# Fewer, longer rows for four small loads, and an earlier clearing of semaphores, in a gated attention and MLP decode kernel

## The chip, the core and the metric

The kernel runs on one core of one Trainium2 chip. A core has four compute engines, TensorE (PE, with its weight loads as PEld), VectorE (DVE), ScalarE (ACT) and GpSimd (POOL), a SyncE (SP) that here only issues transfers, and 16 transfer (DMA) engines that move data between the chip's memory and the on-chip buffer of 128 rows (partitions). Everything is 32-bit floating point. The metric is the device time of one execution in microseconds: the median of three runs, 677.85 us before the change (677.72 to 677.86).

## The reference

Two branches share one input of two rows of 448, and a sigmoid gate mixes them.

```python
B, Sq, D = 2, 1, 448          # H, Sk, Dh = 16, 4096, 256;  F = 1792
g = sigmoid((x * gate_w).sum(-1, keepdims=True))
q = (x @ wq).reshape(B, Sq, H, Dh).transpose(0, 2, 1, 3)
p = softmax(einsum("bhqd,bhkd->bhqk", q, k_cache) * Dh ** -0.5)
a = einsum("bhqk,bhkd->bhqd", p, v_cache).transpose(0, 2, 1, 3).reshape(B, Sq, H * Dh) @ wo
r = maximum(x @ w1 + b1, 0)
b = (r * r) @ w2 + b2
out = g * a + (1 - g) * b
```

K and V caches are 134 MB each, wq and wo 7.3 MB each, w1 and w2 3.2 MB each.

## The kernel before

**Rounds.** The 32 pairs of batch and head are worked through in 16 rounds of two heads of one batch. The tile of a round's K (or V) is 128 rows of 64 KB: 64 rows for each head, 64 keys in each row. VectorE multiplies a half of K's tile by q (`times_q`, L404) and sums over the 256 columns (`row_sums`, L409), half after half (`rest`); the maximum goes through TensorE and back (`maximum`, `softmax`), ScalarE takes the exponentials, and TensorE multiplies them with V (`values`) into a bank `po`. The first twelve rounds are a loop on TensorE; the last four are written out by hand (L599 to L661). K has two buffers, kp0 and kp1, and V one, vp; V of round 14 goes to kp0, which K no longer needs then.

**Output projection.** After each group of four heads (a unit), `turn_wide` transposes the heads' outputs through TensorE with the softmax sums folded in (`rl`), and `project` multiplies by wo. wo comes in four loads of four heads each (`load_wo`, L515). For heads 0 to 11 a load is 128 rows of 14336 bytes: a row holds eight successive rows of wo (`HJ` = 8) and the four heads lie in 32 rows each. The last four heads are two units of two heads, done by `turn_narrow` (L500) and `late_wo` (L529); their wo is laid out in 128 rows of two successive wo rows (`NJ` = 2) for each head, four pieces of 3584 bytes to a row. `late` (L526) spreads a product of two rows of 448 over four places of the bank `fin`.

**MLP.** w1 comes at the start; `ffn_turn` and `ffn_square` (L550 to L564) bring the hidden values into rows, add b1 from the tile `b1T` (128 rows of 14 values) and square them; w2 comes last of all, into kp1, in five pieces whose bounds are `W2_CUTS` (14 columns in all, each 1792 bytes of a row), and `late_w2` adds its products to `fin`.

**Start.** ScalarE issues x, gate_w, b2 and b1 (L292 to L295); x, gate_w and b2 lie at the front of kp1 until K of round 1 takes it. SP issues wq and K of round 0, then w1 and K of round 1.

**Order and waits.** `Flow` writes down every operation in program order with what it reads and writes, and derives the waits; each engine runs its own list in order. An operation that waits keeps everything behind it on the same engine waiting, and SP's loads are such a list. Loads have a semaphore of their own by name. `emit` (L118) allocates the semaphores, emits the engines' lists and, last on SP, behind an operation that waits for both output stores (L662), clears all semaphores in one instruction (L168).

**End.** On SP after K of round 15: V of round 14 (L624), wo of heads 12 to 15 (L636), V of round 15 in three pieces (L637, `V_CUTS`), w2 in five (L638). TensorE then does the values of round 14, `late_wo` of heads 12 and 13, the sums, the values of round 15, `turn_narrow` with the first w2 piece's products inside (L655), `late_wo` of heads 14 and 15 and the rest of w2; VectorE copies `fin` out and SP and ScalarE store one batch each (`store`, L615).

Of the kernel before, what the change touches and what calls it, by code (L numbers as in the profile page):

```python
# [23 lines left out]
class Flow:  # L24
# [7 lines left out]
    def __init__(self, nc):  # L32
        self.nc = nc
        self.eng = {PE: nc.tensor, ACT: nc.scalar, DVE: nc.vector, POOL: nc.gpsimd, SP: nc.sync}
        self.order = {e: [] for e in self.eng}
        self.ops = {}
        self.know = {e: {} for e in self.eng}
        self.seen = {}
        self.tokens = {}
        self.body, self.at, self.passes = None, 0, 0  # L40

    @staticmethod
    def span(r):
# [74 lines left out]
    def emit(self):  # L118
        nc = self.nc
        sems = {}  # L120
        counts = {}
        for proc, ops in self.ops.items():
            at = 0
            for o in ops:
                if proc not in self.eng:
                    o.inc = not o.give
                if o.inc and not o.give:
                    at += 1 if proc in self.eng else 16
                counts[id(o)] = at
        assert all(not t for t in self.tokens.values())  # L130

        def sem(name):
            if name not in sems:
                sems[name] = nc.alloc_semaphore(f"s_{name}")
            return sems[name]

        for proc in self.ops:
            sem(proc)
        for t in self.tokens:
            sem(t)  # L140

        def one(o):
            e = self.eng[o.eng]
            for t, n in o.takes:
                e.wait_ge(sem(t), n).then_inc(sem(t), -n)  # L145
            for p in o.waits:
                e.wait_ge(sem(p.proc), counts[id(p)])  # L147
            i = o.fn()
            n = 1 if o.proc in self.eng else 16
            if o.give:  # L150
                i.then_inc(sem(o.give), n)
            elif o.inc:
                i.then_inc(sem(o.proc), n)

        for eng in (POOL, DVE, ACT, SP, PE):
            for o in self.order[eng]:
                if isinstance(o, Op):
                    one(o)
                else:
                    passes, body, slot = o  # L160
                    with nc.Fori(0, passes, engines=bass.OrderedEngineSet([TYPES[PE]]),
                                 head_slot=None if slot is None else {TYPES[PE]: slot}):
                        for p in body:
                            one(p)
            if eng == SP:
                nums = sorted(s.num for s in sems.values())
                assert nums == list(range(nums[0], nums[0] + len(nums)))
                nc.sync.sem_clear(range(nums[0], nums[0] + len(nums)))  # L168


def gated_mix_kernel(nc, x, k_cache, v_cache, wq, wo, w1, b1, w2, b2, gate_w, out):
    P = 128
    B, H, S, DH = k_cache.shape
    D = x.shape[-1]
# [14 lines left out]
    NQ = N // QB  # L189
    assert QB == 2 * DH  # L190
    DQ = D // 4
    W2_CUTS = (2, 8, 11, 13)
    V_CUTS = (32, 56)
    LEAD = 4
    HJ = HG * DH // P
    HP = P // HG
    HN = HG * DH
    HALF = J * DH
# [3 lines left out]
    op = flow.op  # L202

    def sb(name, *shape):
        return nc.alloc_sbuf_tensor(name, shape, F32).ap()
# [12 lines left out]
    rs_t = [sb(f"rs{n}", P, B * HG) for n in range(2)]  # L218
    eo = sb("eo", P, 2)
    m16 = sb("m16", P, 4 * HG)  # L220
    xT = sb("xT", P, 2, XC, 2, B)
    z = sb("z", B, 1)
    g = sb("g", B, 1)
# [12 lines left out]
    rc = sb("rc", P, HG, B)  # L236
    rl_t = [sb(f"rl{n}", P, HG * B, 2) for n in range(2)]
    oTw = sb("oTw", P, HJ, B)
    oTn = [sb(f"oTn{n}", P, NJ, 2 * B) for n in range(2)]

    po_t = [bank(f"po{n}") for n in range(2)]
    acc = bank("acc")
# [3 lines left out]
    sm = bank("sm")  # L246
# [5 lines left out]
    def load(eng, sem, dst, src, w, r=(), give=None):  # L252
        e = flow.eng[eng]
        op(eng, lambda: e.dma_start(dst, src), r=r, w=w, dma=sem, give=give)  # L254

    def place(t, lo=0, hi=NK * DH):
        return ("vp" if t is vp else "kp1" if t is kp[1] else "kp0", lo, hi)
# [29 lines left out]
    def at_start(k, n=1):  # L287
        return place(kp[1], k * D, (k + n) * D)
# [3 lines left out]
    load(ACT, "x", x2, x.rearrange("b s d -> b (s d)"), [at_start(0)])  # L292
    load(ACT, "gw", gw, gate_w[None, :].to_broadcast([B, D]), [at_start(1)])
    load(ACT, "b2", b2r, b2[None, :].to_broadcast([B, D]), [at_start(2)])
    load(ACT, "b1", b1T, b1.rearrange("(p c) -> p c", c=FC), ["b1T"])  # L295

    v_, s_, t_, g_ = nc.vector, nc.scalar, nc.tensor, nc.gpsimd

# [7 lines left out]
    def vec(fn, r, w, give=None):  # L306
        op(DVE, fn, r=r, w=w, give=give)
# [10 lines left out]
    vec(lambda: v_.tensor_reduce(eo, ident.rearrange("p (a s) -> p s a", s=2), axis=AX.X, op=ALU.add), ["ident"], ["eo"])  # L318
    vec(lambda: v_.tensor_reduce(m16, ident.rearrange("p (r k) -> p k r", r=4)[:, :4 * HG, :], axis=AX.X, op=ALU.add),
        ["ident"], ["m16"])  # L320

    xr = start_at[:, 4 * D:].rearrange("b (k r s) -> b k r s", k=XC, s=2)
    for s in range(2):
# [6 lines left out]
    def mms(calls):  # L330
        def run():
            for out_, lhsT, rhs, start, stop in calls:
                i = t_.matmul(out_, lhsT, rhs, start=start, stop=stop, skip_group_check=True)  # L333
            return i
        return run
# [24 lines left out]
    op(PE, mms([(sm[:, :2 * B], ones_pp[:B, :], gd.rearrange("k s b -> k (s b)"), True, True)]), r=["ones", "gd"], w=["sm"])  # L360
    vec(lambda: v_.tensor_copy(gP, sm[:, :2 * B].rearrange("p (s b) -> p s b", b=B)), ["sm"], ["gP"])
    op(PE, mms([(acc[:B, :D], gd[:, 1, :], b2r, True, False)]), r=["gd", at_start(2)], w=["acc"])

    load_k(0)

# [117 lines left out]
    def turn_wide(u):  # L483
# [12 lines left out]
        for k in range(HG):  # L496
            at = slice(k * HP, (k + 1) * HP)
            op(ACT, lambda k=k, at=at: s_.activation(oTw[at], ptv[at, :, B * k:B * k + B], AF.Copy), r=["sm"], w=[("oTw", k, k + 1)])  # L498

    def turn_narrow(u, between=lambda: None):  # L500
        ptv = sm[:, :NJ * 2 * B].rearrange("p (j c) -> p j c", c=2 * B)
        a = u - NG + 1
        po, name, rl, oT = po_t[u % 2], f"po{u % 2}", rl_t[u % 2], oTn[a]
        o = shared[:, a * 512:(a + 1) * 512]
        op(ACT, lambda: s_.activation(o, po, AF.Copy), r=[name], w=[("shared", a * 512, (a + 1) * 512)])
        between()
        ov = o.rearrange("r (s p j) -> r s j p", s=2, j=NJ)
        op(PE, mms([(ptv[:, j, :], ov[:, s, j, :], rl[:, :2 * B, s], s == 0, s == 1) for j in range(NJ) for s in range(2)]),
           r=[("shared", a * 512, (a + 1) * 512), f"rl{u % 2}"], w=["sm"])
        op(ACT, lambda: s_.activation(oT, ptv, AF.Copy), r=["sm"], w=[f"oTn{a}"])  # L510

    wo_v = wo.rearrange("(h p j) n -> p h (j n)", p=P, j=NJ)
    wo_g = wo.rearrange("(g p j) n -> g p (j n)", p=P, j=HJ)

    def load_wo(u):  # L515
        if u < NG - 1:
            load(SP, "wo", wo_t, wo_g[u], ["wo"])
        else:
            load(SP, "wo", wo_t.rearrange("p (h k) -> p h k", h=HG), wo_v[:, u * HG:(u + 1) * HG, :], ["wo"])

    def project(u):
        t = wo_t.rearrange("p (j n) -> p j n", j=HJ)
# [3 lines left out]
    def late(lt, rhs, start=False, stop=False):  # L526
        return [(fin[32 * k:32 * k + B, :DQ], lt, rhs[:, k * DQ:(k + 1) * DQ], start, stop) for k in range(4)]

    def late_wo(h):  # L529
        u, k = unit_of[h]  # L530
        t = wo_t.rearrange("p (h j n) -> p h j n", h=HG, j=NJ)
        calls = []
        for j in range(NJ):
            calls += late(oTn[u - NG + 1][:, j, B * k:B * k + B], t[:, h % HG, j, :])
        op(PE, mms(calls), r=[f"oTn{u - NG + 1}", "wo"], w=["fin"])

    w2_t = kp[last % 2][:, :FC * D].rearrange("p (c n) -> p c n", n=D)
    w2_v = w2.rearrange("(p c) n -> p c n", c=FC)
# [89 lines left out]
    softmax(i + 1)  # L628
    times_q(i + 2, 0, LEAD, J)
    values(i, vt)  # L630
    turn_narrow(NG - 1)

    i = last - 1
    vt = vt_next
    rest(i + 1, 0, J)
    load_wo(NG - 1)  # L636
    vt_next = load_v(i + 1, vp, V_CUTS)  # L637
    load_w2()  # L638
    values(i, vt, 0, NK // 4)
# [3 lines left out]
    y0 = sb("y0", P, DQ)  # L643
    vec(lambda: v_.tensor_copy(y0, fin[:, :DQ]), ["fin"], ["y0"])
    store(y0, "y0")
    late_wo(H - 4)
    late_wo(H - 3)
    sums(NG)
    norm(NG)

# [1 line left out]
    at = [0, *(c // 2 for c in V_CUTS), NK // 2]  # L652
    for lo, hi in zip(at, at[1:]):
        values(last, vt, lo, hi)
    turn_narrow(NG, lambda: late_w2(0, W2_CUTS[0]))  # L655
    late_wo(H - 2)
    late_wo(H - 1)
    late_w2(W2_CUTS[0], FC)
    y4 = shared[:, :DQ]
    vec(lambda: v_.tensor_copy(y4, fin[:, :DQ]), ["fin"], [("shared", 0, DQ)])  # L660
    store(y4, ("shared", 0, DQ))  # L661
    op(SP, lambda: nc.sync.nop(), r=["out0", "out1"])  # L662
    flow.emit()


# [24 lines left out]
```

## Time and profile before

| What | us |
|---|---|
| median of three runs (lowest, highest) | 677.85 (677.72, 677.86) |
| the profiled execution's own time | 677.82 |
| its span on the core | 676.5 |
| VectorE, TensorE, ScalarE busy in it | 570.2, 245.4, 42.3 |

Times in the profile count from the start of the span; what the profiled execution took beyond its span, 1.32 us, lies around it. In a timeline a row is: start, duration, engine, line, operation, output<-input, shape and count, and in brackets how long the engine had been idle and what ended that. An engine's name with q (SPq, ACTq) is its sequencer, here issuing a transfer. In the groups by line a row has the count, then the busy time in all and the mean of one in ns, then the idle time before. In a table of stretches a row has the bounds, the length, busy time and count for each engine, the granted TensorE clock, the mean busy share of the 16 transfer engines (above 1 where packets overlap) and the rate. q1 is SP's queue of transfers, q10 ScalarE's, q8 the one that brings instructions. Where all matmuls go through one helper they have one line, L333, and are told apart by their tiles.

### The profile page before, as it was taken

How to read it: one execution, taken by the hardware profiler on the slowest of the kernel's cores; microseconds unless marked ns; L12 is line 12 of the kernel's file. 1: busy time of each engine (PE TensorE's matmuls, PEld its weight loads, DVE VectorE, ACT ScalarE, POOL GpSimd, SP SyncE). 2: the span in 40 equal slices, each digit the busy share in tenths (PEclk: the TensorE clock that was granted, in tenths of full speed). 3: DMA queues.
4: the chain of work that ended last, by engine and by line, in shares of the span. 5: the costliest groups of instructions: out<-in, count | busy, mean ns of one | idle time of the engine just before them, and what ended most of it. 6: DMA issues, size and time to landing. Idle time of an engine off the chain costs nothing.

```text
span 676.5 us, 3789 instructions
## 1 busy us (share of the span) xinstructions
PE 245.4 (36%) x1658; PEld 83.3 (12%) x1658; DVE 570.2 (84%) x143; ACT 42.3 (6%) x141; POOL 0.7 (0%) x6
## 2 busy tenths in 40 slices
PE   2522350502305761140505456050411580412476
PEld 1100210100001410010101411010100140100122
DVE  3069999999999895979979896897979899999920
ACT  0001000010100201010000201000010110000000
POOL 0000000000000000000000000000000000000000
PEclk9957585655758577585756678575665765675889
DMA  9999999999999999999999999999999999999997
GB/s 381 426 438 435 435 434 434 434 434 434 434 434 434 419 435 434 434 434 434 434 434 434 457 431 434 434 434 434 430 434 430 401 460 434 434 434 434 392 439 304
DMA packets 7062, 289.71 MB, mean 428 GB/s; under 512 B 902, under 2 KB 1036, under 8 KB 1932
## 3 DMA queue, kind: packets, MB, share of 16 engines
q1 hardware_dynamic: 6880, 289.54, 99.3%
q8 instruction: 8, 0.13, 0.1%
q10 hardware_dynamic: 172, 0.02, 0.0%
q14 instruction: 2, 0.02, 0.0%
HBM read 289.56 MB, written 0.01 MB: 428 GB/s over the span
## 4 chain that ended last, share of the span: by engine, by line
DMA 48%; DVE 31%; PE 3%; SPq 1%; issue 0%; DVEq 0%
DMA kp<-in_A_k_cache_dram 32%; DVE s L409 15%; DVE kp L404 15%; DMA vp<-in_A_v_cache_dram 11%; DMA kp<-in_B_w_dram 5%; PE po L333 3%; SPq L254 1%; PE fin L333 0%; PE mt L333 0%; DVE shared L660 0%; DVEq L147 0%; DVE nb L431 0%
## 5 line engine op out<-in xcount | busy, mean ns | idle before, releaser
L404 DVE TENSOR_TENSOR kp<-kp,q 128x8192 f32<-128x8192 f32 (+2 forms) x34 | 278.2, 8183 | 57.6 <-DMA kp<-in_A_k_cache_dram 57.6
L409 DVE TENSOR_REDUCE s<-kp 128x32 f32<-128x8192 f32 x32 | 278.0, 8686 | 1.1
L333 PE MATMUL po<-vp,pw 128*16 128x512 f32 (+1 forms) x960 | 135.8, 728 | 233.0 <-PEq L145 208.9
L333 PEld LDWEIGHTS po<-vp,pw 128*16 128x16 f32 (+1 forms) x960 | 31.1, 110 | 333.5 <-issue 307.3
L333 PE MATMUL mt<-ident,m 128*64 128x64 f32 x64 | 7.3, 318 | 141.3 <-PEq L145 87.4
L333 PE MATMUL sm<-rl,shared 128*128 128x8 f32 (+1 forms) x112 | 23.6, 347 | 9.2 <-ACT shared L489 8.1
L333 PE MATMUL acc<-wo,oTw 128*2 128x448 f32 x48 | 24.8, 683 | 2.5 <-ACT oTw L498 2.5
L333 PEld LDWEIGHTS sm<-rl,shared 128*128 128x128 f32 x112 | 23.0, 311 | 10.8 <-DVE rl L462 4.6
L450 ACT ACTIVATE pw<-zero 128x128 f32<-128x128 f32 x12 | 3.7, 312 | 325.5 <-PE po L333 325.5
L333 PEld LDWEIGHTS mt<-ident,m 128*64 128x64 f32 x64 | 4.8, 191 | 155.0 <-issue 99.0
L438 ACT ACTIVATE pw<-s,nb 64x64 f32<-64x64 f32 x32 | 11.1, 348 | 169.8 <-DVE nb L431 169.6
L660 DVE COPY shared<-fin 128x112 f32<-128x112 f32 x1 | 0.3, 275 | 20.8 <-PE fin L333 20.8
L333 PE MATMUL ph<-vp,xT 128*4 128x448 f32 x28 | 8.2, 759 | 15.6 <-DMA vp<-in_B_w_dram 15.6
L333 PE MATMUL po<-kp,pw 128*8 128x512 f32 x64 | 9.4, 744 | 8.8 <-DMA kp<-in_A_v_cache_dram 8.8
L333 PE MATMUL pq<-qs,sel 128*64 128x256 f32 x48 | 12.3, 594 | 0.0
L431 DVE TENSOR_REDUCE nb<-mt 128x1 f32<-128x64 f32 x16 | 3.6, 224 | 9.8 <-PE mt L333 9.8
L333 PE MATMUL po<-vp,xT 128*4 128x512 f32 x56 | 8.7, 787 | 4.9 <-DMA vp<-in_A_wq_dram 4.9
L460 DVE RECIPROCAL rc<-sm 128x8 f32<-128x8 f32 (+1 forms) x5 | 1.0, 196 | 7.7 <-PE sm L333 7.7
L380 ACT ACTIVATE q<-pq 128x256 f32<-128x256 f32 x16 | 6.1, 383 | 21.0 <-PE pq L333 20.7
L489 ACT ACTIVATE shared<-po 128x512 f32<-128x512 f32 x12 | 6.5, 591 | 11.4 <-PE sm L333 11.4
L333 PEld LDWEIGHTS acc<-wo,oTw 128*2 128x2 f32 x48 | 4.5, 98 | 20.6 <-issue 17.8
L438 ACT ACTIVATION_READ_ACCUMULATOR pw<-s,nb 64x1 f32 x32 | 5.9, 184 | 0.0
(65 smaller groups left out, 66.2 us busy)
## 6 DMA issues: line engine op xcount, KB each, us to landing
vp<-in_A_wq_dram SPq DMA_DIRECT2D x1, 7168.0 KB, 19.4
wo<-in_A_wo_dram SPq DMA_DIRECT2D x4, 1792.0 KB, 45.2
vp<-in_A_v_cache_dram SPq DMA_DIRECT2D x1, 4096.0 KB, 24.8
vp<-in_B_w_dram SPq DMA_DIRECT2D x1, 3136.0 KB, 18.0
vp<-in_A_v_cache_dram SPq DMA_DIRECT2D x1, 3072.0 KB, 31.7
kp<-in_B_w_dram SPq DMA_DIRECT2D x1, 1344.0 KB, 37.1
vp<-in_A_v_cache_dram SPq DMA_DIRECT2D x1, 1024.0 KB, 33.7
kp<-in_B_w_dram SPq DMA_DIRECT2D x2, 448.0 KB, 33.5
```

The lines of the kernel that those rows point to most:

```text
L254: op(eng, lambda: e.dma_start(dst, src), r=r, w=w, dma=sem, give=give)
L333: i = t_.matmul(out_, lhsT, rhs, start=start, stop=stop, skip_group_check=True)
L380: op(ACT, lambda: s_.activation(t, pq[:, :DH], AF.Copy), r=["pq"], w=[f"q{i % 3}"])
L404: vec(lambda: v_.tensor_tensor(kt, kt, q.unsqueeze(1).to_broadcast([P, hi - lo, DH]), op=ALU.mult), at + [f"q{i % 3}"], at)
L409: vec(lambda: v_.tensor_reduce(s[:, at], rows(t)[:, at, :], axis=AX.X, op=ALU.add), [place(t, half * HALF, (half + 1) * HALF)], [(f"s{i % ...
L431: vec(lambda: v_.tensor_reduce(nb, mt[:, :PH], axis=AX.X, op=ALU.max, negate=True), ["mt"], [f"nb{i % 2}"])
L438: op(ACT, lambda: s_.activation(pw[at, :, 2 * c:2 * c + 2], s[at].rearrange("p (m s) -> p m s", s=2), AF.Exp, bias=nb[at], accum_out=rs[at ...
L450: op(ACT, lambda: s_.activation(at, zero.unsqueeze(2).unsqueeze(3).to_broadcast([P, NK // 2, 2, 2]), AF.Copy), r=["zero"], w=[("pw0", 2 * ...
L460: vec(lambda: v_.reciprocal(c, sm[:, :B * n].rearrange("p (k b) -> p k b", b=B)), ["sm"], ["rc"])
L489: op(ACT, lambda s=s, lo=lo: s_.activation(o_w[:, s], pv[:, s, lo:lo + HJ // 2].unsqueeze(2).to_broadcast([P, HJ // 2, HG, HP]), AF.Copy), ...
L660: vec(lambda: v_.tensor_copy(y4, fin[:, :DQ]), ["fin"], [("shared", 0, DQ)])
```

## The change

Four parts:

- wo of heads 12 and 13 is loaded by itself, as 64 rows of 14336 bytes, in the layout of the earlier units (`load_wo`, u = 3). A new `turn_half` transposes these two heads into 64 rows (`oT2`), and `late_half` multiplies: eight steps on 64 rows instead of four on 128. wo of heads 14 and 15 keeps its layout and goes to kp1 behind w2's place (`wo_e`), free once the first half of K of round 15 has been reduced.
- b1 is loaded as 16 rows of 448 bytes to the front of kp1; one matmul with a mask `e16` repeats each row over eight partitions, and VectorE picks each partition's 14 values with a second mask `m_i` (a product and a sum) into `b1T`.
- w2 comes in four pieces, of 8, 3, 2 and 1 columns, and all its products come after those of wo.
- All semaphores but those of the two output stores are cleared while the stores are under way; ScalarE counts up a marker, `acted`, as its last instruction, which SP waits for; the stores' own two semaphores are waited for and counted down behind it.

```diff
-        for proc in self.ops:
-            sem(proc)
+        ends = [p for p in self.ops if p in self.last]
+        for proc in self.ops:
+            if proc not in ends:
+                sem(proc)
         for t in self.tokens:
             sem(t)
+        sem("acted")
+        inner = sorted(s.num for s in sems.values())
+        assert inner == list(range(inner[0], inner[0] + len(inner)))
+        for proc in ends:
+            sem(proc)
...
+            if eng == ACT:
+                nc.scalar.nop().then_inc(sem("acted"), 1)
             if eng == SP:
-                nums = sorted(s.num for s in sems.values())
-                assert nums == list(range(nums[0], nums[0] + len(nums)))
-                nc.sync.sem_clear(range(nums[0], nums[0] + len(nums)))
+                nc.sync.wait_ge(sem("acted"), 1)
+                nc.sync.sem_clear(range(inner[0], inner[0] + len(inner)))
+                for proc in ends:
+                    n = 16 * len(self.ops[proc])
+                    nc.sync.wait_ge(sem(proc), n).then_inc(sem(proc), -n)
...
-    W2_CUTS = (2, 8, 11, 13)
+    W2_CUTS = (8, 11, 13)
...
-    load(ACT, "b1", b1T, b1.rearrange("(p c) -> p c", c=FC), ["b1T"])
+    BR = 16
+    BI = P // BR
+    b1_at = 4 * D + XC * P
+    b1r = kp[1][:BR, b1_at:b1_at + BI * FC]
+    e16 = kp[1][:BR, b1_at + BI * FC:b1_at + BI * FC + P]
+    b1w = kp[1][:, b1_at + BI * FC + P:b1_at + 2 * BI * FC + P]
...
+    load(ACT, "b1", b1r, b1.rearrange("(r n) -> r n", r=BR), [b1r_at])
...
+    vec(lambda: v_.tensor_reduce(m_i, ident.rearrange("p (a i) -> p i a", i=BI), axis=AX.X, op=ALU.add), ["ident"], ["m_i"])
+    vec(lambda: v_.tensor_copy(e16.rearrange("r (a i) -> r a i", i=BI), ident[:BR, :BR].unsqueeze(2).to_broadcast([BR, BR, BI])),
+        ["ident"], [e16_at])
...
+    op(PE, mms([(ph[:, :BI * FC], e16, b1r, True, True)]), r=[e16_at, b1r_at], w=["ph"])
+    vec(lambda: v_.tensor_tensor(b1w.rearrange("p (c i) -> p c i", i=BI), ph[:, :BI * FC].rearrange("p (i c) -> p c i", i=BI),
+                                 m_i.unsqueeze(1).to_broadcast([P, FC, BI]), op=ALU.mult), ["ph", "m_i"], [b1w_at])
+    vec(lambda: v_.tensor_reduce(b1T, b1w.rearrange("p (c i) -> p c i", i=BI), axis=AX.X, op=ALU.add), [b1w_at], ["b1T"])
...
+    def turn_half():
+        u = NG - 1
+        ptv = sm[:PH, :HJ * 2 * B].rearrange("p (j c) -> p j c", c=2 * B)
+        po, rl = po_t[u % 2], rl_t[u % 2]
+        o_h = shared.rearrange("r (s j k p) -> r s j k p", s=2, j=HJ, k=2)
+        pv = po.rearrange("r (s p j) -> r s j p", s=2, j=HJ)
+        for s in range(2):
+            op(ACT, lambda s=s: s_.activation(o_h[:, s], pv[:, s].unsqueeze(2).to_broadcast([P, HJ, 2, HP]), AF.Copy),
+               r=[f"po{u % 2}"], w=[("shared", s * HN // 2, (s + 1) * HN // 2)])
+        ov = o_h.rearrange("r s j k p -> r s j (k p)")
+        op(PE, mms([(ptv[:, j, :], ov[:, s, j, :], rl[:, :2 * B, s], s == 0, s == 1) for j in range(HJ) for s in range(2)]),
+           r=["shared", f"rl{u % 2}"], w=["sm"])
+        for k in range(2):
+            at = slice(k * HP, (k + 1) * HP)
+            op(ACT, lambda k=k, at=at: s_.activation(oT2[at], ptv[at, :, B * k:B * k + B], AF.Copy), r=["sm"], w=[("oT2", k, k + 1)])
...
+    wo_e = kp[last % 2][:, FC * D:FC * D + 2 * NJ * D].rearrange("p (h j n) -> p h j n", h=2, j=NJ)
...
         if u < NG - 1:
             load(SP, "wo", wo_t, wo_g[u], ["wo"])
+        elif u < NG:
+            load(SP, "wo", wo_t[:PH], wo_g[u, :PH], ["wo"])
         else:
-            load(SP, "wo", wo_t.rearrange("p (h k) -> p h k", h=HG), wo_v[:, u * HG:(u + 1) * HG, :], ["wo"])
+            load(SP, "wo_e", wo_e.rearrange("p h j n -> p h (j n)"), wo_v[:, H - 2:, :], [wo_e_at])
...
+    def late_half():
+        t = wo_t[:PH].rearrange("p (j n) -> p j n", j=HJ)
+        calls = []
+        for j in range(HJ):
+            calls += late(oT2[:, j, :], t[:, j, :])
+        op(PE, mms(calls), r=["oT2", "wo"], w=["fin"])
...
-    turn_narrow(NG - 1)
+    turn_half()
...
     load_wo(NG - 1)
+    load_wo(NG)
     vt_next = load_v(i + 1, vp, V_CUTS)
     load_w2()
...
-    late_wo(H - 4)
-    late_wo(H - 3)
+    late_half()
...
-    turn_narrow(NG, lambda: late_w2(0, W2_CUTS[0]))
-    late_wo(H - 2)
-    late_wo(H - 1)
-    late_w2(W2_CUTS[0], FC)
+    turn_narrow(NG)
+    late_wo(0)
+    late_wo(1)
+    late_w2(0, FC)
...
-    op(SP, lambda: nc.sync.nop(), r=["out0", "out1"])
```

More of the change, by code (lines that the diff above doesn't have):

```diff
@@ L40, in __init__ @@
         self.body, self.at, self.passes = None, 0, 0
+        self.last = ("out0", "out1")
     @staticmethod
@@ L220, in gated_mix_kernel @@
     m16 = sb("m16", P, 4 * HG)
+    m_i = sb("m_i", P, 8)
     xT = sb("xT", P, 2, XC, 2, B)
@@ L238, in gated_mix_kernel @@
     oTw = sb("oTw", P, HJ, B)
-    oTn = [sb(f"oTn{n}", P, NJ, 2 * B) for n in range(2)]
+    oT2 = sb("oT2", P // 2, HJ, B)
+    oTn = sb("oTn", P, NJ, 2 * B)
     po_t = [bank(f"po{n}") for n in range(2)]
@@ L294, in gated_mix_kernel @@
     load(ACT, "b2", b2r, b2[None, :].to_broadcast([B, D]), [at_start(2)])
-    load(ACT, "b1", b1T, b1.rearrange("(p c) -> p c", c=FC), ["b1T"])
+    BR = 16
[4 more added lines that the diff above has]
+    b1w = kp[1][:, b1_at + BI * FC + P:b1_at + 2 * BI * FC + P]
+    b1r_at = place(kp[1], b1_at, b1_at + BI * FC)
+    e16_at = place(kp[1], b1_at + BI * FC, b1_at + BI * FC + P)
+    b1w_at = place(kp[1], b1_at + BI * FC + P, b1_at + 2 * BI * FC + P)
+    load(ACT, "b1", b1r, b1.rearrange("(r n) -> r n", r=BR), [b1r_at])
     v_, s_, t_, g_ = nc.vector, nc.scalar, nc.tensor, nc.gpsimd
@@ L498, in turn_wide @@
             op(ACT, lambda k=k, at=at: s_.activation(oTw[at], ptv[at, :, B * k:B * k + B], AF.Copy), r=["sm"], w=[("oTw", k, k + 1)])
+    def turn_half():
[13 more added lines that the diff above has]
+            op(ACT, lambda k=k, at=at: s_.activation(oT2[at], ptv[at, :, B * k:B * k + B], AF.Copy), r=["sm"], w=[("oT2", k, k + 1)])
     def turn_narrow(u, between=lambda: None):
         ptv = sm[:, :NJ * 2 * B].rearrange("p (j c) -> p j c", c=2 * B)
[L502 to L505, printed above, removed]
+        po, name, rl = po_t[u % 2], f"po{u % 2}", rl_t[u % 2]
+        o = shared[:, 512:1024]
+        op(ACT, lambda: s_.activation(o, po, AF.Copy), r=[name], w=[("shared", 512, 1024)])
         between()
@@ L508, in turn_narrow @@
         op(PE, mms([(ptv[:, j, :], ov[:, s, j, :], rl[:, :2 * B, s], s == 0, s == 1) for j in range(NJ) for s in range(2)]),
-           r=[("shared", a * 512, (a + 1) * 512), f"rl{u % 2}"], w=["sm"])
-        op(ACT, lambda: s_.activation(oT, ptv, AF.Copy), r=["sm"], w=[f"oTn{a}"])
+           r=[("shared", 512, 1024), f"rl{u % 2}"], w=["sm"])
+        op(ACT, lambda: s_.activation(oTn, ptv, AF.Copy), r=["sm"], w=["oTn"])
     wo_v = wo.rearrange("(h p j) n -> p h (j n)", p=P, j=NJ)
     wo_g = wo.rearrange("(g p j) n -> g p (j n)", p=P, j=HJ)
+    wo_e = kp[last % 2][:, FC * D:FC * D + 2 * NJ * D].rearrange("p (h j n) -> p h j n", h=2, j=NJ)
+    wo_e_at = place(kp[last % 2], FC * D, FC * D + 2 * NJ * D)
+    assert FC * D + 2 * NJ * D <= HALF
     def load_wo(u):
@@ L527, in late, with late_wo @@
         return [(fin[32 * k:32 * k + B, :DQ], lt, rhs[:, k * DQ:(k + 1) * DQ], start, stop) for k in range(4)]
-    def late_wo(h):
-        u, k = unit_of[h]
-        t = wo_t.rearrange("p (h j n) -> p h j n", h=HG, j=NJ)
+    def late_half():
[4 more added lines that the diff above has]
+        op(PE, mms(calls), r=["oT2", "wo"], w=["fin"])
+    def late_wo(k):
         calls = []
         for j in range(NJ):
-            calls += late(oTn[u - NG + 1][:, j, B * k:B * k + B], t[:, h % HG, j, :])
-        op(PE, mms(calls), r=[f"oTn{u - NG + 1}", "wo"], w=["fin"])
+            calls += late(oTn[:, j, B * k:B * k + B], wo_e[:, k, j, :])
+        op(PE, mms(calls), r=["oTn", wo_e_at], w=["fin"])
     w2_t = kp[last % 2][:, :FC * D].rearrange("p (c n) -> p c n", n=D)
```

## The prediction

> **What bounds the kernel now.** I read the page first, its slices and its queues.
>
> ```profile
> span 676.5 us, 3789 instructions
> PE 245.4 (36%) x1658; PEld 83.3 (12%) x1658; DVE 570.2 (84%) x143; ACT 42.3 (6%) x141; POOL 0.7 (0%) x6
> DMA  9999999999999999999999999999999999999997
> DMA packets 7062, 289.71 MB, mean 428 GB/s; under 512 B 902, under 2 KB 1036, under 8 KB 1932
> q1 hardware_dynamic: 6880, 289.54, 99.3%
> q8 instruction: 8, 0.13, 0.1%
> ```
>
> The transfer engines are at nine tenths or more in 39 slices of 40. The load queue q1 alone keeps them occupied for 99.3% of 676.5 us, that is 671.8 us, while VectorE, the busiest compute engine, has 570 us of work. So the kernel is bound by its loads: a change counts if it shortens or stalls that stream, or the work behind its last byte. Two stretches show the full rate and the end of the stream; the columns after the four engines' busy times are POOL, the TensorE clock, the DMA share and GB/s.
>
> ```profile
> 60.00:226.00 166.00, 50.37 (x370) 18.72 (x370) 159.68 (x37) 9.53 (x36) 0.00 (x0) 0.61 1.00 434
> 670.00:674.00 4.00, 3.14 (x112) 2.02 (x100) 0.00 (x0) 0.00 (x0) 0.00 (x0) 1.00 0.60 234
> ```
>
> Steady loading runs at 434 GB/s. In the last stretch 234 GB/s x 4 us = 936 KB still move, which is 2.16 us of full rate. The tail, in order of time, shows what follows:
>
> ```profile
> 666.10 0.20 PEld L333 LDWEIGHTS po<-vp,pw 128*8 128x8 f32 x8 [0.66 <-DMA vp<-in_A_v_cache_dram]
> 667.30 0.60 ACT L505 ACTIVATE shared<-po 128x512 f32<-128x512 f32 x1 [17.94 <-PE po L333]
> 669.38 0.95 PE L333 MATMUL fin<-wo,oTn 128*2 128x112 f32 x32 [0.27 <-ACT oTn L510]
> 670.47 1.33 PE L333 MATMUL fin<-kp,hT 128*2 128x112 f32 x48
> 673.28 0.86 PE L333 MATMUL fin<-kp,hT 128*2 128x112 f32 x24 [0.38 <-DMA kp<-in_B_w_dram]
> 673.77 0.11 PEld L333 LDWEIGHTS fin<-kp,hT 128*2 128x2 f32 x8 [0.19 <-DMA kp<-in_B_w_dram]
> 674.21 0.28 DVE L660 COPY shared<-fin 128x112 f32<-128x112 f32 x1 [20.80 <-PE fin L333]
> 674.51 0.51 SPq L254 DMA_DIRECT2D out_dram<-shared  x1
> ```
>
> TensorE waits for the last w2 piece until 673.77; then come eight matmuls, one copy and the store. The 2.16 us of bytes end at 673.77 rather than 672.16, so a mean transfer engine is done up to 1.6 us before the last one. The q8 row fits: 0.1% of 16 engines' span for eight instruction packets is 676.5 x 0.001 x 16 / 8 = 1.4 us per packet (0.7 to 2.0 by its rounding), and each sits on one engine. It is the last engine that sets the end.
>
> The end itself is in two rows, the final wait and the clear, and in the wait for the stores:
>
> ```profile
> L662 SPq EVENT_SEMAPHORE  x1: 17/17/17, 676.4 to 676.4; - x1
> L168 SPq EVENT_SEMAPHORE_RANGE_CLEAR  x1: 78/78/78, 676.4 to 676.4; - x1
> SPq L662 <- DMA out_dram<-shared: 1.3, 1, 1.3
> ```
>
> **The packets.** Bytes stay the same; rows get longer. wo of heads 12 and 13 goes from 2 x 128 rows of 3584 bytes to 64 of 14336: 192 packets fewer. w2's first two pieces become one: 128 fewer. b1 goes from 128 rows to 16: 112 fewer. Completion packets: one w2 load less, one wo load more, nothing. That is 432 packets, 27 per engine. The price of a packet is not in the trace directly, so I bound it: 289.54 MB at 434 GB/s is 667.1 us, q1 was occupied for 671.8, and the 4.7 us between, over 6880/16 = 430 packets, give at most 11 ns each. The other bound is nothing, since the next packet may be fetched under the one before. So 0 to 27 x 11 ns = 0.30 us. I take 0.20, nearer the upper end, because little but the packets can fill the 4.7 us.
>
> **The 64-row load.** It moves half of a wo load.
>
> ```profile
> wo<-in_A_wo_dram SPq DMA_DIRECT2D x4, 1792.0 KB, 45.2
> b1T<-in_B_b_dram ACTq DMA_DIRECT2D x1, 7.0 KB, 30.3
> ```
>
> 896 KB are 0.918 MB, 2.11 us at 434 GB/s. No load of this size on half of the rows stands in the trace; the nearest short ones, x, gate and b2 on two rows, say nothing of its rate. Bounds: it runs at the full rate (0), or at half of it (2.11 us more, less what the early engines absorb). I take 0, by the nearest row, wo's other loads, which lie within the full rate; the other end is the first rival. [...]
>
> **The extra work on chip.** The rows around it:
>
> ```profile
> 629.03 8.68 DVE L404 TENSOR_TENSOR kp<-kp,q 128x8192 f32<-128x8192 f32 x1
> 631.49 1.29 SPq L254 DMA_DIRECT2D vp<-in_A_v_cache_dram  x3
> 631.49 0.60 ACT L505 ACTIVATE shared<-po 128x512 f32<-128x512 f32 x1 [17.71 <-PE po L333]
> 632.23 1.08 PE L333 MATMUL sm<-rl,shared 128*128 128x4 f32 x8 [0.82 <-ACT shared L505]
> 642.09 5.81 PE L333 MATMUL po<-kp,pw 128*8 128x512 f32 x32 [8.78 <-DMA kp<-in_A_v_cache_dram]
> 651.53 0.95 PE L333 MATMUL fin<-wo,oTn 128*2 128x112 f32 x32
> 652.41 0.39 PE L333 MATMUL sm<-rs,ones_pp 128*128 128x4 f32 x2
> 656.32 5.32 PE L333 MATMUL po<-vp,pw 128*8 128x512 f32 x32 [3.53 <-DMA vp<-in_A_v_cache_dram]
> L333 PE MATMUL sm<-rl,shared 128*128 128x8 f32 (+1 forms) x112 | 23.6, 347 | 9.2 <-ACT shared L489 8.1 <-ACT shared L505 1.1
> ```
>
> turn_half copies twice on ScalarE instead of once, 0.60 us more, and issues 16 calls (32 matmuls) instead of 4 (8): by the 632.23 row 32 x 0.135 = 4.3 us, by the group's mean 32 x 0.21 = 6.7 us. From 632.8 it ends between 637.1 and 639.5. TensorE next waits for V of round 14 until 642.09, so at least 2.6 us of cover remain. late_half issues 64 matmuls instead of 32: 1.9 us instead of 0.95, behind which stand sums and norm and then the first piece of the last V at 656.32. The sums now end at 652.8; 0.95 later is 653.8, cover 2.5 us. Whatever either took beyond its cover would delay the values behind it, and through them, at most one for one, the end.
>
> SP's queue gets one more instruction that waits: the load of heads 14 and 15 goes into the first half of K's last tile and waits for its reduction, which ends where the 629.03 product starts. Behind it stand the three V loads, which wait for TensorE until 631.49 anyway. A load issue is 1.29/3 = 0.43 us, so it is out by 629.5: 2.0 us of cover. If that went, V15 and w2 would be issued later, and the stream still has V14, in use only from 642.09, to work on.
>
> At the tail the 16 w2 matmuls that ran inside the turn now follow the head's 32. By the 670.47 row one is 1.33/48 = 28 ns; 104 of 112 from 670.4 end at 673.3, before the last piece is there at 673.77. Cost nothing, cover 0.5 us.
>
> **b1 on chip.** Rows of the start:
>
> ```profile
> 9.41 0.61 DVE L354 SCALAR_TENSOR_TENSOR kp<-kp 2x448 f32<-2x448 f32 x1 [2.25 <-DMA kp<-in_gate_w_dram]
> 13.73 1.65 PE L333 MATMUL acc<-kp,gd 2*2 2x448 f32 x2 [2.39 <-DMA kp<-in_B_b_dram]
> 20.23 8.70 PE L333 MATMUL po<-vp,xT 128*4 128x512 f32 x56 [4.85 <-DMA vp<-in_A_wq_dram]
> 29.00 0.33 SPq L254 DMA_DIRECT2D vp<-in_B_w_dram  x1
> 39.62 8.69 DVE L404 TENSOR_TENSOR kp<-kp,q 128x8192 f32<-128x8192 f32 x1 [28.08 <-DMA kp<-in_A_k_cache_dram]
> L318 DVE TENSOR_REDUCE eo<-ident 128x2 f32<-128x128 f32 x1 | 0.3, 275 | 0.0
> ```
>
> The two new masks cost VectorE about 0.28 + 0.28 us by L318, ahead of a 2.25 us wait for gate_w: free. Landings on ScalarE's queue follow one another by 13.73 - 9.41 = 4.3 us, so a b1 with few rows should land near 18.0; the old one, with 128, landed at 1.9 + 30.3 = 32.2. Its matmul, product and sum (about 0.6 + 0.28 + 0.28) then fit before 20.23 on TensorE, and long before 39.62 on VectorE. The reload of K's tile, whose start b1 now borrows, is issued behind the 29.00 load. All of it costs nothing. If b1 landed late, the wq matmuls behind it would be late, then w1's load; the stream has K of round 0 until 39.62, so the price starts when w1 is issued past that, with b1 landing after 39.6 - 8.7 - 0.7 = 30.2 (8.7 for the wq matmuls, 0.7 for b1's own matmul and the issue).
>
> **The end.** The clear (78 ns) and ScalarE's extra marker run while the stores fly (1.3 us of cover; SP's new wait for the marker has only the clear and the last waits behind it, for which nobody waits but the end). Behind the last landing stand two waits with a decrement, 17 ns each by L662, in place of one wait and the clear: 61 ns less, between 0 and 0.1 (676.5 - 676.4). I take 0.06.
>
> **Sum.** Profiled time 677.82 (span 676.5 and 1.32 around it): 677.82 - 0.20 - 0.06 = 677.56; the median is 0.03 above the profiled run: **677.6**.
>
> **Rivals.** *One: the 64-row load runs at half rate.* [...] For it: nothing in the kernel has filled half of the rows with so much, and each engine's share of 434 GB/s is never exceeded in a long stretch. [...]
>
> *Two: the instruction packets fall elsewhere.* The program grows by turn_half's and late_half's calls. A 1.4 us packet on the last engine gives 677.6 + 1.4 = 679.0; one that spares it, 676.2. For it: q8's eight packets and the spread; against: eight packets over sixteen engines need not meet.
>
> *Three: b1 lands late,* at 32.2 as before: 2.0 us past the point above, 679.6. Against: 16 rows queue less than 128.
>
> *Four: nothing is gained.* Packets overlap wholly: 677.8.
>
> **How the numbers follow.** Chances: forecast 0.50, one 0.32, two 0.08 (half each way), three 0.03, four 0.07. A measurement of this kernel can tell about 0.2%, 1.36 us, from no change: below 676.5 is faster, above 679.2 slower. Slower: half of rival one, three, and part of two and of what I have not seen: 0.23. Faster: the lucky half of two and the unseen: 0.07. The rest, 0.70, is the same. The range goes from 677.0 to 679.4; the likeliest case's own is 677.4 to 677.9.
>
> **What would show it.** Right: q1 near 6560 packets (less 192 and 128), steady 434 GB/s, the last w2 wait 0.2 us earlier, the clear before the last waits, TensorE's waits at 642, 656 and 20.2 still on loads. Wrong: a dip of GB/s to near half for some microseconds where the 64 rows move, around 642 to 648, and every later landing late by one amount; a wait of the wq matmuls on b1; a tail whose matmuls no longer wait for w2.

## The result, and the profile after

The changed kernel takes 683.07 us (median of six runs, 682.50 to 683.54) beside 677.84 us for the kernel before in the same comparison (677.60 to 677.86): a ratio of 1.0078, 95% interval 1.0065 to 1.0091, 5.2 us slower. The forecast was 677.6, the range ended at 679.4.

The page of the changed kernel (profiled execution 683.24 us), its span, transfers and slices of 681.6/40 = 17.04 us:

```profile
span 681.6 us, 3914 instructions
DMA  9999999999999999999999999999999999999996
GB/s 378 473 424 438 439 431 431 431 431 427 435 431 408 443 435 431 431 438 446 446 431 435 423 428 431 431 431 435 438 431 431 446 436 431 435 431 428 298 429 279
DMA packets 6630, 289.71 MB, mean 425 GB/s; under 512 B 790, under 2 KB 924, under 8 KB 1436
q1 hardware_dynamic: 6560, 289.54, 99.1%
q8 instruction: 8, 0.13, 0.1%
```

The same rates of the kernel before, in slices of 16.91 us:

```profile
GB/s 381 426 438 435 435 434 434 434 434 434 434 434 434 419 435 434 434 434 434 434 434 434 457 431 434 434 434 434 430 434 430 401 460 434 434 434 434 392 439 304
```

The packets are the 6560 of the forecast. The engines are as busy as before (a 9 for slice 38 in both), yet that slice moves 298 GB/s where it moved 392: here the busy share does not show the rate. Closer, in stretches of 4 and 24 us, first the changed kernel, then the kernel before (columns as in the prediction):

```profile
640.00:644.00 4.00, 0.00 (x0) 0.00 (x0) 4.00 (x1) 0.00 (x0) 0.00 (x0) 0.50 0.77 145
644.00:648.00 4.00, 2.88 (x16) 0.59 (x20) 2.49 (x2) 0.00 (x0) 0.00 (x0) 0.50 0.97 224
636.00:660.00 24.00, 11.41 (x136) 3.73 (x135) 11.38 (x8) 1.22 (x6) 0.00 (x0) 0.71 0.99 342
```

```profile
640.00:644.00 4.00, 1.91 (x12) 0.44 (x16) 4.00 (x1) 0.00 (x0) 0.00 (x0) 0.50 0.88 351
644.00:648.00 4.00, 4.00 (x28) 0.75 (x20) 2.65 (x2) 0.00 (x0) 0.00 (x0) 0.68 1.14 481
636.00:660.00 24.00, 14.39 (x122) 3.83 (x126) 11.54 (x8) 0.88 (x4) 0.00 (x0) 0.72 0.97 411
```

Over 24 us the stream lost (411 - 342) x 24 / 434 = 3.8 us. Between 640 and 648, where the 64 rows move, it lost (351 + 481 - 145 - 224) x 4 / 434 = 4.3 us, more than the whole; the rest of the 24 us moved a little more than before. This fall of the rate is called the dip below. Rows picked from the timeline of the changed kernel around and behind it:

```profile
628.98 0.39 SPq L268 DMA_DIRECT2D kp<-in_A_wo_dram  x1
632.58 1.29 SPq L268 DMA_DIRECT2D vp<-in_A_v_cache_dram  x3
633.81 2.35 PE L360 MATMUL sm<-rl,shared 128*64 128x4 f32 x32 [1.31 <-ACT shared L539]
645.12 5.47 PE L360 MATMUL po<-kp,pw 128*8 128x512 f32 x32 [8.95 <-DMA kp<-in_A_v_cache_dram]
...
654.34 1.71 PE L360 MATMUL fin<-wo,oT 64*2 64x112 f32 x64
...
667.98 3.62 PE L360 MATMUL po<-vp,pw 128*8 128x512 f32 x32 [1.08 <-DMA vp<-in_A_v_cache_dram]
...
673.75 0.95 PE L360 MATMUL fin<-kp,oTn 128*2 128x112 f32 x32 [0.27 <-ACT oTn L557]
674.76 2.21 PE L360 MATMUL fin<-kp,hT 128*2 128x112 f32 x76
678.26 1.13 PE L360 MATMUL fin<-kp,hT 128*2 128x112 f32 x36 [1.29 <-issue]
679.43 0.28 DVE L717 COPY shared<-fin 128x112 f32<-128x112 f32 x1 [22.45 <-PE fin L360]
679.73 0.52 SPq L268 DMA_DIRECT2D out_dram<-shared  x1
```

Three things are to be seen. V of round 14 lands at 645.12 instead of 642.09, although it stands ahead of the 64 rows in SP's queue. The last wo products start at 673.75 instead of 669.38: 4.37 us, the stream's delay carried unchanged to the tail. And the copy starts at 679.43 instead of 674.21, 5.22 us later, so the tail adds 0.85: TensorE stands still for 1.29 us among the w2 products, waiting for nothing that the profile shows ("issue").

The start and the end of the changed kernel, from its timeline and from the group of the clear:

```profile
18.11 0.76 PE L360 MATMUL ph<-kp 16*128 16x112 f32 x2 [2.64 <-DMA kp<-in_B_b_dram]
18.90 0.28 DVE L392 TENSOR_TENSOR kp<-ph,m_i 128x112 f32<-128x112 f32 x1 [7.35 <-PE ph L360]
19.21 0.27 DVE L394 TENSOR_REDUCE b1T<-kp 128x14 f32<-128x112 f32 x1
20.22 8.18 PE L360 MATMUL po<-vp,xT 128*4 128x512 f32 x56 [1.35 <-DMA vp<-in_A_wq_dram]
```

```profile
L177 SPq EVENT_SEMAPHORE_RANGE_CLEAR  x1: 84/84/84, 680.3 to 680.3; - x1
```

b1 landed at 18.1 and its three steps ended before the wq products at 20.22. The clear runs in the shadow of the stores, and the way from the copy to the span's end is 681.6 - 679.43 = 2.17 us, before 676.5 - 674.21 = 2.29.

### The profile page after: what moved, and what is told of

It is laid out like the page before. It is cut to its first block, busy times and chain, and to the rows that moved or that the text cites. A ratio compares the mean times of both kernels' runs of the same rounds, so it can differ in the third digit from the quotient of the medians.

```text
span 681.6 us, 3914 instructions
## 1 busy us (share of the span) xinstructions
PE 250.0 (37%) x1716; PEld 86.5 (13%) x1716; DVE 571.2 (84%) x147; ACT 42.9 (6%) x143; POOL 0.7 (0%) x6
## 3 DMA queue, kind: packets, MB, share of 16 engines
q1 hardware_dynamic: 6560, 289.54, 99.1%
## 4 chain that ended last, share of the span: by engine, by line
DMA 49%; DVE 31%; PE 3%; issue 0%; SPq 0%; DVEq 0%
DMA kp<-in_A_k_cache_dram 32%; DVE s L441 15%; DVE kp L436 15%; DMA vp<-in_A_v_cache_dram 11%; DMA kp<-in_B_w_dram 6%; PE po L360 3%; PE fin L360 0%; SPq L268 0%; PE mt L360 0%; DVE shared L717 0%; DVEq L155 0%; DVE nb L463 0%
## 5 line engine op out<-in xcount | busy, mean ns | idle before, releaser
L360 PE MATMUL po<-vp,pw 128*16 128x512 f32 (+1 forms) x960 | 138.3, 740 | 231.9 <-PEq L153 207.9
L360 PE MATMUL sm<-rl,shared 128*128 128x8 f32 (+2 forms) x136 | 24.8, 320 | 10.2 <-ACT shared L521 8.1
L360 PEld LDWEIGHTS sm<-rl,shared 128*128 128x128 f32 (+1 forms) x136 | 24.2, 282 | 12.5 <-DVE rl L494 4.6
```

## The experiments

Fifteen runs were made, in four groups, each group beside the kernel before on the same chip (677.93, 677.95, 677.92 and 678.01 us). Letters of theories are those of the expectations.

### Which part costs

**Without the 64 rows.** The change, with `turn_narrow(NG - 1)`, one `load_wo(NG - 1)` of 128 rows and `late_wo` as before.

```diff
-    turn_half()
+    turn_narrow(NG - 1)
...
-    load_wo(NG)
...
-    late_half()
+    late_wo(H - 4)
+    late_wo(H - 3)
```

> The whole change without its 64-row part: wo of heads 12 to 15 as before, with b1, w2 and the semaphores as changed. Theory A (the 64-row load drags the whole stream at half rate for as long as any transfer engine is in it, about 4.2 us, and about 1 us more is TensorE waiting for its own instructions in the last matmuls because w2's products now come in one burst): 677.6 without the TensorE wait, 678.6 with it. Theory B (the 64-row load costs its own 2.1 us only, the other 3 come from b1, w2 or the end): 680 to 681.

678.47 us, ratio 1.0015 [1.0005, 1.0025], no dip (417 GB/s from 636 to 660). 4.6 of the 5.2 us are gone with the 64 rows, but the runs scatter from 677.61 to 680.13, and half a microsecond stays.

**w2 as before.** The change, with w2 in five pieces and the first piece's products inside the turn.

```diff
-    W2_CUTS = (8, 11, 13)
+    W2_CUTS = (2, 8, 11, 13)
...
-    turn_narrow(NG)
+    turn_narrow(NG, lambda: late_w2(0, W2_CUTS[0]))
...
-    late_w2(0, FC)
+    late_w2(W2_CUTS[0], FC)
```

> The whole change with w2 as before (five pieces, the first one's products inside the last turn). Theory A: the dip of the rate stays, the TensorE wait of 1.3 us before the last 36 w2 matmuls goes, 682.1. Theory A' (the wait comes from the longer code of the 64-row part, not from w2's order): 683.1. Theory B: below 681.

682.77 us (681.86 to 683.22), ratio 1.0071 [1.0055, 1.0088]. The dip stays (345 GB/s from 636 to 660). Its tail waits for w2 again and has no issue gap:

```profile
675.28 1.33 PE L360 MATMUL fin<-kp,hT 128*2 128x112 f32 x48
676.90 0.76 PE L360 MATMUL fin<-kp,hT 128*2 128x112 f32 x24 [0.28 <-DMA kp<-in_B_w_dram]
677.98 0.92 PE L360 MATMUL fin<-kp,hT 128*2 128x112 f32 x24 [0.32 <-DMA kp<-in_B_w_dram]
```

**The 64 rows alone.** The kernel before with only `turn_half`, `late_half` and the two loads of the change (diff as in the change's description).

> The kernel before with the 64-row part alone. Theory A: 677.85 + 4.2 = 682.0, with packets of 14336 bytes at half their rate and about 8 us of the stream near 217 GB/s. Theory B: 680.0.

683.23 us, ratio 1.0078 [1.0061, 1.0095]: 5.3 us, as much as the whole change. Theory A's 4.2 was too low. In the profiles so far that hold this load, the second piece of the last V comes at 667.98 (the change), 668.42 (w2 as before) and 669.28 (here) where it came at 663.61: 4.4 to 5.7 us late.

**The same load in 128 rows.** w2 as before, and wo of heads 12 and 13 in 128 rows of 7168 bytes; the turn goes to 128 rows in four steps.

```diff
-            load(SP, "wo", wo_t[:PH], wo_g[u, :PH], ["wo"])
+            load(SP, "wo", wo_t[:, :MJ * D], wo_m[u * P * HJ // (P * MJ)], ["wo"])
```

> The change with w2 as before, and wo of heads 12 and 13 in 128 rows of 7168 bytes instead of 64 rows of 14336: the same bytes, the same two loads, the same place in the queue, a turn and products of the same form on 128 rows. Theory A (the rows that are filled are the cause): no dip, 677.4 to 677.7. Rival C (a second wo load, its wait in SP's queue or the new turn and products are the cause, not the rows): 680 or more.

677.72 us (677.55 to 677.98), ratio 0.9997 [0.9987, 1.0007]. The row of 636 to 660:

```profile
636.00:660.00 24.00, 14.64 (x126) 3.93 (x130) 11.28 (x8) 0.88 (x4) 0.00 (x0) 0.73 0.98 417
```

The same bytes, from the same place in the queue, cost nothing in 128 rows. This kernel, with b1 and the clear in it, is about 0.2 us under the kernel before, which the interval can't tell from no change.

### What it is in the 64 rows

**Half of each row.** As the run with w2 as before, but only the first 7168 bytes of each of the 64 rows are loaded: half of the wo of heads 12 and 13 stays out.

```diff
-            load(SP, "wo", wo_t[:PH], wo_g[u, :PH], ["wo"])
+            load(SP, "wo", wo_t[:PH, :HJ * D // 2], wo_g[u, :PH, :HJ * D // 2], ["wo"])
```

> As the run with w2 as before (682.8), but the 64-row load brings only the first half of each row, 64 rows of 7168 bytes; the other half of wo of heads 12 and 13 is left out, 0.46 MB or 1.06 us of full rate less. Theory A (the half rate lasts from the first transfer engine's entry to the last one's exit, so the spread between engines is paid whatever the size): the loss falls from 5.05 to about 4.0, 677.7 - 1.06 + 4.0 = 680.7. Rival G (the loss goes with the bytes): 677.7 - 1.06 + 2.5 = 679.2.

679.65 us (678.98 to 681.21). The 128-row kernel with 0.459 MB less would take 677.72 - 1.06 = 676.66, so the loss is 3.0 us: between the two theories, and no decision.

**An extra load at the start.** The kernel before, with one more load of 0.918 MB ahead of K of round 0, in rows 0 to 63, then in 128 rows. Nothing reads it.

```diff
+    load(SP, "wox", wo_t[:PH], wo.rearrange("(g p j) n -> g p (j n)", p=P, j=HJ)[3, :PH], ["wo"])
     load_k(0)
```

```diff
+    load(SP, "wox", wo_t[:, :HJ * D // 2], wo.rearrange("(g p j) n -> g p (j n)", p=P, j=HJ // 2)[6], ["wo"])
     load_k(0)
```

> The kernel before with one load more: the same 64 rows of 14336 bytes of wo, issued at the start behind wq and K of round 0, into wo's tile, where nobody reads them before wo's first load overwrites them. Its own bytes are 2.11 us at 434 GB/s: 677.95 + 2.11 = 680.06 without any loss. At that point the transfer engines are 0.44 us apart instead of 1.9. Theory A (half rate for as long as any engine is in the load, so loss = half of (0.918 MB and what the others move meanwhile) / 217 GB/s): about 2.3 to 2.7 us of loss, 682.4 to 682.8. Rival G (a loss fixed by the bytes, 4.7 to 5 us here): 684.8 to 685.1.

> As the run before it, with the same bytes in 128 rows of 7168 bytes. Theory A and rival G alike (the filled rows are the cause): no loss beyond the bytes, 680.0. Rival H (a load more at that place costs by its wait or its issue): as much as the 64-row one.

682.94 us with 64 rows (ratio 1.0073 [1.0056, 1.0090]) and 680.19 with 128 (1.0033 [1.0021, 1.0046]). The extra bytes cost 680.19 - 677.92 = 2.27 us, the rows 0 to 63 another 2.75. The stretches of the first and of the second:

```profile
38.00:42.00 4.00, 0.00 (x0) 0.00 (x0) 1.19 (x1) 0.00 (x0) 0.00 (x0) 0.50 0.94 208
34.00:50.00 16.00, 0.00 (x0) 0.00 (x0) 9.15 (x2) 0.00 (x0) 0.00 (x0) 0.50 0.96 343
```

```profile
38.00:42.00 4.00, 0.00 (x0) 0.00 (x0) 2.26 (x1) 0.00 (x0) 0.00 (x0) 0.50 0.94 399
34.00:50.00 16.00, 0.68 (x2) 0.10 (x4) 10.23 (x2) 0.00 (x0) 0.00 (x0) 0.50 0.98 422
```

208 GB/s is half of 434 within 5%, with the transfer engines just as busy (0.94). At this place the load costs what half the rate says (2.11 us) and 0.6 more. Theory A had 2.3 to 2.7 for it; theory G, which had 4.7 to 5, falls.

**Other rows, same number and length.** The extra load into rows 32 to 95 instead of 0 to 63:

```diff
+    load(SP, "wox", wo_t[32:96], wo.rearrange("(g p j) n -> g p (j n)", p=P, j=HJ)[3, :PH], ["wo"])
     load_k(0)
```

> The kernel before with the same extra load of 64 rows of 14336 bytes at the start as in the run with rows 0 to 63, but into rows 32 to 95. [...] Theory L (few rows or long ones: 64 rows of 14336 bytes are slow wherever they go): 38 to 42 near 208 GB/s again, time 682.8 to 683.1.

680.02 us (679.83 to 680.33), ratio 1.0030 [1.0019, 1.0041], as with 128 rows, and no dip:

```profile
38.00:42.00 4.00, 0.00 (x0) 0.00 (x0) 2.16 (x1) 0.00 (x0) 0.00 (x0) 0.50 0.95 405
34.00:50.00 16.00, 0.61 (x2) 0.10 (x4) 10.13 (x2) 0.00 (x0) 0.00 (x0) 0.51 0.99 426
```

And in its place at the end, with w2 as before, into every second row; the products then read old data in half of the rows.

```diff
-            load(SP, "wo", wo_t[:PH], wo_g[u, :PH], ["wo"])
+            load(SP, "wo", wo_t[0:P:2], wo_g[u, :PH], ["wo"])
```

> The change with w2 as before, whose 64-row load of heads 12 and 13 goes to every second row (0, 2, ..., 126) instead of rows 0 to 63; the products still read rows 0 to 63, so half of them read old data. [...] Theory L: dip as before near 342, time 682 to 683.

677.70 us, ratio 0.9996 [0.9986, 1.0006], 418 GB/s from 636 to 660. In other places sixty-four rows of 14336 bytes run as fast as the same bytes in 128 rows, at the start (405 GB/s beside 399) and at the end (418 beside 417). Theory L falls: few rows and long rows are out as a cause, and the place is what counts.

### The tail

**The w2 part alone.** The kernel before with the change's `W2_CUTS` and its order of products; timed once, and profiled two more times in executions of their own.

```diff
-    W2_CUTS = (2, 8, 11, 13)
+    W2_CUTS = (8, 11, 13)
...
-    turn_narrow(NG, lambda: late_w2(0, W2_CUTS[0]))
+    turn_narrow(NG)
...
-    late_w2(W2_CUTS[0], FC)
+    late_w2(0, FC)
```

> The kernel before with the w2 part alone: four pieces, all of w2's products behind wo's. Theory D (the unsteady 677.6 to 680.1 of the run without the 64-row part comes from TensorE running through more matmuls without a pause in the tail and reaching instructions that have not arrived): again unsteady, single times from 677.8 to 680.2, median 678.3 to 678.8. Rival E (b1 or the clearing makes it unsteady): steady at 677.8.

> The kernel with the w2 part alone once more, for a profile of a long execution. Theory D: where the time is near 680.1, TensorE's w2 matmuls stand for 1 to 2 us waiting for nothing but issue, at the end of an instruction packet of q8; where it is near 677.7, they do not.

> The same kernel and the same expectation a third time: a gap for issue among the w2 matmuls if the time is near 680.1, none if it is near 677.7.

678.46 us, ratio 1.0015 [1.0005, 1.0024], from 677.59 to 680.15, where 31 runs of the kernel before lie between 677.65 and 678.35. The profiled execution of the timed runs took 677.75, the other two 678.77 and 680.10: three different tails of one program. The rows show the clock of the first execution; then the clock of the second and its burst (the 112 products of w2 in one go); then the third's last values and its burst:

```profile
670.00:672.00 2.00, 1.93 (x80) 1.55 (x69) 0.00 (x0) 0.00 (x0) 0.00 (x0) 1.00 0.87 339
672.00:674.00 2.00, 1.70 (x56) 0.90 (x48) 0.00 (x0) 0.00 (x0) 0.00 (x0) 1.00 0.20 78
```

```profile
670.00:672.00 2.00, 1.95 (x56) 1.39 (x48) 0.00 (x0) 0.00 (x0) 0.00 (x0) 0.63 0.88 342
672.00:674.00 2.00, 2.00 (x52) 1.58 (x44) 0.00 (x0) 0.00 (x0) 0.00 (x0) 0.51 0.20 77
```

```profile
670.57 4.48 PE L333 MATMUL fin<-kp,hT 128*2 128x112 f32 x112
```

```profile
663.66 5.32 PE L333 MATMUL po<-vp,pw 128*8 128x512 f32 x32 [1.98 <-DMA vp<-in_A_v_cache_dram]
...
672.43 3.99 PE L333 MATMUL fin<-kp,hT 128*2 128x112 f32 x112
```

At a granted clock of 0.63 and 0.51 the 112 products take 4.48 us and end at 675.05, 0.9 us after the first tail's copy started at 674.14. In the third run the last values ran near half clock as well (granted 0.62 and 0.52 from 664 to 668; 5.32 us, at full clock 3.62), and the burst starts 1.9 us later. No stretch of "issue" stands in either: the theory that the instructions weren't there falls for these runs. What sets the clock is not settled. The clock records of these traces have only 0.5 and 1.0, and the half level begins at other times in each execution (from 670.53 to 673.94 in the second, from 671.32 to 674.73 in the third, 3.41 us in both; in the first the granted clock is 1.00 from 664 to 674). Why the half level falls on the burst in some executions no run here shows.

**The order alone, and the pieces alone.** Five pieces with the products after wo's; and four pieces cut (2, 11, 13) with the order of before.

```diff
-    turn_narrow(NG, lambda: late_w2(0, W2_CUTS[0]))
+    turn_narrow(NG)
...
-    late_w2(W2_CUTS[0], FC)
+    late_w2(0, FC)
```

```diff
-    W2_CUTS = (2, 8, 11, 13)
+    W2_CUTS = (2, 11, 13)
```

> The kernel before with w2 in its five pieces, but all products behind wo's (the first piece's 16 matmuls leave the turn). Theory D: the order is the cause, unsteady up to 680, median 678.3 to 678.8. Rival F (the number or size of the pieces is the cause): steady at 677.9.

> The kernel before with w2 in four pieces of 2, 9, 2 and 1 columns and the order of the products as before. Theory D: steady at 677.8 to 677.9. Rival F: unsteady, median 678.3 or more.

678.17 us (ratio 1.0006 [0.9996, 1.0015]) and 678.36 (1.0009 [0.9999, 1.0018]), each with one run of ten near 680.1. Neither is told apart from no change. Against the expectations, the first lies between theory D's 678.3 and rival F's 677.9, and the second is at F's 678.3 or more, not at D's 677.8 to 677.9: no theory gets both. The burst of the first and of the second:

```profile
671.95 2.87 PE L333 MATMUL fin<-kp,hT 128*2 128x112 f32 x112
```

```profile
672.17 2.48 PE L333 MATMUL fin<-kp,hT 128*2 128x112 f32 x96 [1.74 <-DMA kp<-in_B_w_dram]
```

In the first the values had run late, and TensorE, no longer the data, ends the kernel: 26 ns for each of 112 products at full clock. In the second a piece of nine columns lands as a whole, 1.74 us after TensorE is free for it, and 96 products are left to do.

**The changed kernel once more.** No edit.

> The changed kernel once more, for the gap of 1.29 us in the last w2 products that the first profile puts down to issue. If the gap belongs to the program (instructions that are not there yet whenever the tail is late): again 1 us or more of issue in the fin matmuls, TensorE clock 1.00. If it was chance: no such gap, and the time is 682 to 683 with the dip alone.

684.76 us, one run, above the six timed. No issue gap, but the burst near half clock (granted 0.64 and 0.51 from 676 to 680), and the stream still later (second piece of the last V at 669.77, in the first profile 667.98):

```profile
676.57 4.49 PE L360 MATMUL fin<-kp,hT 128*2 128x112 f32 x112
681.14 0.28 DVE L717 COPY shared<-fin 128x112 f32<-128x112 f32 x1 [21.48 <-PE fin L360]
```

So the gap of 1.29 us does not belong to every execution of the program. What it was stays open. In the first profile's packet records an instruction packet of 16 KB (q8) runs from 675.75 to 676.82, just before the gap begins at 676.97; but the kernel before has one from 671.54 and the w2 part alone has one from 671.12, 671.10 and 672.73, in the last products too, without such a gap.

## Why the prediction was wrong

**The step that failed: "I take 0, by the nearest row, wo's other loads".** Those rows have the same bytes per row but fill 128 rows; the new load fills rows 0 to 63. The runs with rows 32 to 95 and with every second row show that the place alone makes the difference. The row I leaned on was near in size and far in the one property that decides. At the start the stretch shows 208 GB/s for rows 0 to 63, 405 for rows 32 to 95 and 399 for 128 rows. I gave rival one, the load at half rate, 0.32.

**Its rival had the rate and the wrong size.** My price for rival one was 0.5 to 2.1 us: the 2.11 us of half rate, less up to 1.6, the spread between the engines, as a credit. The credit was my estimate, and no run shows it. The load cost 2.75 us at the start, and 5.3 by itself at the end, where the second piece of the last V was 4.4 to 6.2 us late in four profiles. Nothing was credited: packets of V that were still under way beside the 64 rows took longer. The single packets of the trace show it. A packet of the 64 rows takes 1.09 us (the median), where one of the same size into every second row takes 0.54. A 64 KB packet of V takes 2.42 us, and none of V of round 14 took over 2.97 in the kernel before; in the changed kernel, where the first packet of the 64 rows starts at 639.34, the last eight, started from 637.95 to 639.01, took 3.07 to 4.70. So V of round 14, ahead in the queue, landed 3.03 us late, in the stretch in which the rate had fallen to 145 and 224 GB/s.

In the kernel before, the engines end their last V packet up to 2 us apart (639.70 to 641.60), and at the start their last K packet about half a us apart (38.72 to 39.17). That this spread is what makes 5 of 2.75 fits, but the spread was not varied alone; and what holds up the V packets beside the 64 rows no run here shows.

**The second step that failed: "Cost nothing, cover 0.5 us" for w2.** 28 ns for a product is a price at full clock (1.00 from 670 to 674). Three differences size the part: 0.30 us (change against change with w2 as before), 0.75 (678.47 against 677.72), 0.51 (alone), between medians of scattered runs. Near half clock (0.63 and 0.51, 0.64 and 0.51) the 112 products took 4.48 and 4.49 us in two profiles, and the cover of 0.5 is gone. In the order before, 16 of them ran while ScalarE copied and TensorE waited. Two profiled executions show what that is worth: both had the last values near half clock (0.51 and 0.63, 0.53 and 0.62 from 664 to 668) and the products of w2 at full clock (1.00 from 670 to 676), the 128-row kernel with the order before, and then the five pieces with the products behind wo's.

```profile
663.59 5.32 PE L361 MATMUL po<-vp,pw 128*8 128x512 f32 x32 [2.00 <-DMA vp<-in_A_v_cache_dram]
671.82 2.48 PE L361 MATMUL fin<-kp,hT 128*2 128x112 f32 x96
```

```profile
663.72 5.32 PE L333 MATMUL po<-vp,pw 128*8 128x512 f32 x32 [2.00 <-DMA vp<-in_A_v_cache_dram]
```

They took 677.98 and 678.48. Of the 0.50 us between them 0.13 is a later V; the rest is near the 0.39 by which 2.87 us for 112 products exceed 2.48 for 96.

**What held.** The packets: 6560. Their gain of 0.20, and the clear's 0.06, stay unproven: the 128-row kernel, with b1, the clear and part of the saving (6768 packets on q1), lies 0.2 us under the kernel before, which its interval can't tell from nothing. The waits: SP issued the second half of wo at 628.98, 3.6 us before V's pieces became free to go at 632.58. turn_half took 2.35 us for its 32 products where 4.3 to 6.7 were allowed, late_half 1.71 against 1.9. b1: 18.11 against 18.0. The end: 0.12 us shorter against 0.06, within the rounding of the spans. Rival three (b1 late) fell by the row at 18.11. Rival two has little for it: q8 has eight packets as before, of 1.0 to 1.1 us each instead of the estimated 1.4, and one of them lies in the last stretch in both kernels (from 671.54 and from 675.75); which engine carries them the trace doesn't say. None of this decided the result.

The "would be wrong" part named the dip near half the rate between 642 and 648 and a common delay behind it; it came from 640 to 648, and the loads behind it were late by about 4.4 us. Its other sign, a tail whose matmuls no longer wait for w2, came too: the gap in the first profile, the burst at half clock in the second.

## What to carry to other kernels

A load is priced by which rows it fills as well as by its bytes: the same 0.918 MB went at 208 GB/s into rows 0 to 63, and in rows 32 to 95 (405 GB/s) or in every second row (418) cost nothing, so spread a narrow one as in these two runs. Where a row of the trace with the same rows is missing, the dearer end of the bounds is the one to take (here even that, 2.1 us, was too low). The load at half rate in a saturated stream wasn't absorbed by the engines' spread here (5.3 us lost, with engines up to 2 us apart); count what runs beside it too, ahead of it in the queue as well (V of round 14, 3.03 us late). Work that is moved into a last burst on TensorE is to be costed at half clock (4.48 us for the 112 products that took 2.87 at full clock), and left in a gap that exists anyway if the gap is free.

## What the runs showed of the hardware that was not expected

- 0.918 MB into rows 0 to 63 cost 2.75 us over the same bytes in 128 rows at the start, about 5 at the end, and delayed a transfer ahead of it by 3.03 us (eight of that transfer's packets took 3.07 to 4.70 us instead of 2.42); in rows 32 to 95 or in every second row it cost nothing (680.02 and 677.70 us against 680.19 and 677.72 for 128 rows).
- From 640 to 644 the stream fell to 145 GB/s, below half of 434, with the engines' busy share still at 0.77.
- One program's tail ran at a granted TensorE clock of 1.00, of 0.63 and 0.51 (670 to 674), or of 0.62 and 0.52 (664 to 668) and again 0.50 (672 to 674), in three executions, with 2.35 us between the shortest and the longest of them.
- One execution stood still for 1.29 us at full clock for nothing that the profile shows; another execution of the same program did not.
